# Moving the PSUM bank of the last narrow matmul chain of a fused gated mix

## The chip, the cores and the metric

One core of a Trainium2 chip runs the whole kernel. The metric is device time in microseconds (us), smaller is better; runs at full granted clock are compared with one another. The kernel before took 265.14 us (median of three runs, 265.03 to 265.6). Most of the argument reads the trace: the stretch from the first W4 matmul of the last tile to the end of the span, called "the tail stretch" below.

In the views PE stands for the matmuls of TensorE and PEld for its weight loads, DVE for VectorE, ACT for ScalarE, POOL for GpSimd, and SPq for the queue that issues the stores. PSUM is the memory that the matmuls of this kernel write; it is divided into banks. An "evacuation" is the VectorE instruction that reads a finished result from PSUM. A semaphore is a counter through which one engine waits for another.

## The reference

The reference mixes two branches with a sigmoid gate per row: linear attention over 32 heads, and a two-step MLP. What matters here is the end of the second branch and the mix, for S = 2048 rows, D = 640 columns and F = 1728 hidden columns in bfloat16:

```python
x1 = x + hs                                   # (S, 640)
h2 = _gelu(_layernorm(x1, axis=-1) @ w3) @ w4 # (S, 1728) @ (1728, 640)
b  = x1 + h2
return g * a + (1 - g) * b
```

## The kernel before

The kernel goes through the rows in four tiles of 512, and in each tile through four column groups `cc` (0 to 3) of the transposed hidden layer, each giving 128 output rows. One output has 128 x 640 float32; the kernel gives it a PSUM tile of two banks of 512 float32 each, a "pair". All PSUM tiles are such pairs, and their pool has four. Each output is computed as two parts, `hf` 0 and 1, one in each bank. The product with W4 sums over 13 full blocks of 128 hidden columns, and over a remainder of 64, which `w4_rest` computes for two groups at once in the two halves of the array (in the traces two such matmuls start 3 to 4 ns apart).

```python
ps = ctx.enter_context(tc.tile_pool(name="ps", bufs=4, space=PSUM))

def pair():
    return ps.tile([P, 2, 512], F32, name="pp")
# ... cut ...
LT = TS // 2                                                         # 256

def w4_dst(t, cc, pts, hf):
    n = D - TS if t == NT - 1 and cc % 2 else LT                     # 128 or 256
    return (pts[cc][:, 0, TS - n:TS], 0, n) if hf == 0 else (pts[cc][:, 1, 0:D - n], n, D)

def w4_mm(t, cc, pts, hf, start):
    dst, a, b = w4_dst(t, cc, pts, hf)
    for fc in range(FF):                                             # 13 blocks
        nc.tensor.matmul(dst, lhsT=st[t]["h2"][:, fc * TS + cc * P:fc * TS + (cc + 1) * P],
                         rhs=w4_sb[:, fc, a:b], start=start and fc == 0, stop=not start and fc == FF - 1)

def w4_part(t, cc, pts, hf):                                         # last tile, groups 1 and 3
    # ... cut: oc is one output tile per group ...
    nc.vector.scalar_tensor_tensor(oc[:, a:b], src, omg[:, c:c + 1], st[t]["x1"][cc][:, a:b],
                                   op0=ALU.mult, op1=ALU.add)
    nc.sync.dma_start(out2[c * P:(c + 1) * P, a:b], oc[:, a:b])

def w4_tile(t):
    pts = {cc: pair() for cc in (0, 2)}
    # ... cut: both parts of groups 0 and 2, without the remainder ...
    for cc in (1, 3):
        pts[cc] = pair()
    w4_rest(t, pts)                          # ends groups 0 and 2, starts groups 1 and 3
    # ... cut ...
    for cc in (0, 2):
        w4_out(t, cc, pts[cc])               # one evacuation and one store of 640 columns
    last = t == NT - 1
    for cc, hf in ((1, 1), (3, 1), (1, 0), (3, 0)) if last else ((1, 0), (1, 1), (3, 0), (3, 1)):
        # ... cut ...
        w4_mm(t, cc, pts, hf, False)
        if last:
            w4_part(t, cc, pts, hf)
        elif hf == 1:
            w4_out(t, cc, pts[cc])
```

In the last tile groups 1 and 3 are cut into a wide part of 512 columns and a narrow one of 128, and the two narrow parts come last, so that only 128 columns are left to evacuate and store behind the last matmul. "Chain" below means the 13 matmuls of one part.

Of the kernel before, what the change touches and what calls it, by code (L numbers as in the profile page):

```python
# [8 lines left out]
ALU = mybir.AluOpType  # L9
BF16 = mybir.dt.bfloat16  # L10
# [6 lines left out]
def kernel(  # L17
# [13 lines left out]
    nc = tc.nc  # L31
    P = 128
    S, D = A_x.shape[1], A_x.shape[2]
# [3 lines left out]
    TS = 512  # L37
    NT = S // TS
    CPT = TS // P
# [16 lines left out]
    out2 = out.rearrange("b s d -> (b s) d")  # L56
# [8 lines left out]
    outp = ctx.enter_context(tc.tile_pool(name="outp", bufs=2))  # L65
# [3 lines left out]
    def pair():  # L69
        return ps.tile([P, 2, 512], F32, name="pp")  # L70
# [25 lines left out]
    omg = const.tile([P, NCH], F32)  # L96
# [119 lines left out]
    for c in range(1, NCH):  # L216
        pt = pair()
# [175 lines left out]
    st = {}  # L393
# [30 lines left out]
    def x1_scale(t, cc):  # L424
        c = t * CPT + cc
        x1 = st[t]["x1"][cc]
        nc.scalar.activation(x1[:], x1[:], ACT.Copy, scale=omg[:, c:c + 1])
# [11 lines left out]
    LT = TS // 2  # L439
# [15 lines left out]
    def w3_rest(t, dst):  # L455
        for dc in range(DC):
            for v in range(2):
                nc.tensor.matmul(dst[FR * v:FR * (v + 1), :], lhsT=w3_sb[:, dc, FF * P:F],  # L458
                                 rhs=st[t]["lnT"][:, dc, v * LT:(v + 1) * LT], start=(dc == 0), stop=(dc == DC - 1))
        st[t]["h2x"] = h2x_p.tile([P, LT], BF16, name="h2x")  # L460
        nc.scalar.activation(st[t]["h2x"][:], dst, ACT.Gelu_apprx_tanh)  # L461

    def w4_dst(t, cc, pts, hf):
        n = D - TS if t == NT - 1 and cc % 2 else LT
        return (pts[cc][:, 0, TS - n:TS], 0, n) if hf == 0 else (pts[cc][:, 1, 0:D - n], n, D)

    def w4_mm(t, cc, pts, hf, start):
        dst, a, b = w4_dst(t, cc, pts, hf)
        for fc in range(FF):
            nc.tensor.matmul(dst, lhsT=st[t]["h2"][:, fc * TS + cc * P:fc * TS + (cc + 1) * P],  # L470
                             rhs=w4_sb[:, fc, a:b], start=start and fc == 0, stop=not start and fc == FF - 1)

    def w4_rest(t, pts):
        for u in range(2):
            for hf in range(2):
                for v in range(2):
                    rows = slice(FR * v, FR * (v + 1))
                    dst, a, b = w4_dst(t, u + 2 * v, pts, hf)
                    nc.tensor.matmul(dst, lhsT=st[t]["h2x"][rows, u * P:(u + 1) * P],  # L479
                                     rhs=w4_sb[rows, FF, a:b], start=u == 1, stop=u == 0)  # L480

    def w4_out(t, cc, pt):
        c = t * CPT + cc
        x1 = st[t]["x1"][cc]
        oc = outp.tile([P, D], BF16, name="oc")
        nc.vector.scalar_tensor_tensor(oc[:], pt[:].rearrange("p h e -> p (h e)")[:, TS - LT:TS - LT + D],  # L486
                                       omg[:, c:c + 1], x1[:], op0=ALU.mult, op1=ALU.add)
        nc.sync.dma_start(out2[c * P:(c + 1) * P, :], oc[:])

    ocs = {}  # L490

    def w4_part(t, cc, pts, hf):
        c = t * CPT + cc
        src, a, b = w4_dst(t, cc, pts, hf)
        if cc not in ocs:
            ocs[cc] = outp.tile([P, D], BF16, name="oc")
        oc = ocs[cc]
        nc.vector.scalar_tensor_tensor(oc[:, a:b], src, omg[:, c:c + 1], st[t]["x1"][cc][:, a:b],
                                       op0=ALU.mult, op1=ALU.add)
        nc.sync.dma_start(out2[c * P:(c + 1) * P, a:b], oc[:, a:b])  # L500

    def w4_tile(t):
        pts = {cc: pair() for cc in (0, 2)}
        for cc in (0, 2):
            if t + 1 < NT:
                x1_scale(t + 1, cc)
            for hf in range(2):
                w4_mm(t, cc, pts, hf, True)
        for cc in (1, 3):
            pts[cc] = pair()  # L510
        w4_rest(t, pts)
        if t + 1 < NT:
            w3_rest(t + 1, pts[0][:, 0, 0:LT])
        for cc in (0, 2):
            w4_out(t, cc, pts[cc])
        last = t == NT - 1
        for cc, hf in ((1, 1), (3, 1), (1, 0), (3, 0)) if last else ((1, 0), (1, 1), (3, 0), (3, 1)):
            if t + 1 < NT and hf == 0:
                x1_scale(t + 1, cc)
            w4_mm(t, cc, pts, hf, False)  # L520
            if last:
                w4_part(t, cc, pts, hf)
            elif hf == 1:
                w4_out(t, cc, pts[cc])

    for cc in range(CPT):
        w2_unit(0, cc)
# [19 lines left out]
    for t in range(NT):  # L547
        for i in range(NW3):
            w3_unit(t, i)
            if i < CPT and t + 1 < NT:  # L550
                w2_unit(t + 1, i)
            if 2 <= i < 2 + CPT:
                att_unit(t, i - 2)
        if t + 1 < NT:
            ln2_rstd(t + 1, 0, CPT)
            for cc in range(CPT):
                ln2_apply(t + 1, cc)
        if t == 0:
            w3_rest(0, pair()[:, 0, 0:LT])
        w4_tile(t)  # L560
# [30 lines left out]
```

## Time and profile before

| | kernel before |
|---|---|
| time, median of 3 | 265.14 us |
| span of the profiled run | 263.48 us |
| PE busy, share of the span | 98% |
| first W4 matmul of the last tile | 245.45 us |
| tail stretch | 18.03 us |

Lines of the page of the kernel before: busy time of the engines, the TensorE clock in tenths by slices of the span, and the chain of waits.

```profile
PE 258.4 (98%) x1722; PEld 161.0 (61%) x1740; DVE 141.4 (54%) x276; ACT 82.7 (31%) x123; POOL 20.2 (8%) x65
...
PEclk9999999999999999999999999999999999999999
...
PE 92%; SPq 3%; DMA 3%; issue 1%; DVE 0%
```

TensorE bounds the kernel: hardly any stage has a gap on PE. What can still be won lies in small gaps and in the serial tail behind the last matmul.

The timeline of the end of the kernel before. Columns: start, duration from the first start to the last end, engine, line, operation, output and inputs, shape, count, and in brackets the idle time before and what ended it. The timeline merges neighbours, so a row can hold other shapes than the one it names.

```profile
245.45 7.23 PE L470 MATMUL pp<-w_sb,h 128*128 128x256 bf16 x52
...
252.61 0.72 PE L479 MATMUL pp<-w_sb,h2x 64*128 64x256 bf16 x8
253.09 1.68 DVE L486 SCALAR_TENSOR_TENSOR oc<-pp,omg,x 128x640 bf16<-128x640 f32 x2 [7.57 <-PE pp L479]
253.26 6.39 PEld L470 LDWEIGHTS <-h 128*128 128x128 bf16 x40 [0.27 <-issue]
253.49 7.29 PE L470 MATMUL pp<-w_sb,h 128*128 128x512 bf16 x51 [0.16 <-issue]
254.00 1.12 SPq L488 DMA_DIRECT2D out_dram<-oc  x2
256.28 0.75 DVE L498 SCALAR_TENSOR_TENSOR oc<-pp,omg,x 128x512 bf16<-128x512 f32 x1 [1.51 <-PE pp L470]
257.06 4.46 SPq L500 DMA_DIRECT2D out_dram<-oc  x4
259.09 1.08 DVE L498 SCALAR_TENSOR_TENSOR oc<-pp,omg,x 128x512 bf16<-128x512 f32 x2 [2.05 <-PE pp L470]
259.89 0.71 PEld L470 LDWEIGHTS <-h 128*128 128x128 bf16 x12 [0.24 <-issue]
260.81 0.35 DVE L498 SCALAR_TENSOR_TENSOR oc<-pp,omg,x 128x128 bf16<-128x128 f32 x1 [0.65 <-PE pp L470]
```

Read the row at 259.89 first: the weight loads of the last chain stand idle for 0.24 us in the middle of otherwise dense work. By the records of the single instructions the matmuls of a 128-column chain start 56 ns apart, but the last chain's first one starts 336 ns after the one before it, 0.28 us late. It carries a semaphore wait on VectorE in the trace. The row at 259.09 holds two evacuations: that of group 3's wide part (0.75 us, ending at 259.84) and that of group 1's narrow part. The last chain starts 0.05 us after the first of the two ends. PE's own row shows no gap there, because the modelled end of one matmul overlaps the next starts.

The row at 253.49 names an idle 0.16 us that isn't one: it has 51 of 52 matmuls, and with the missing record put in at its place the starts are regular.

### The profile page before, as it was taken

The numbers are of one execution on the slowest core, as the hardware profiler recorded it, in microseconds if no ns is written. First come the engines' busy times: TensorE is split into PE (matmuls) and PEld (weight loads), VectorE is DVE, ScalarE is ACT, GpSimd is POOL, SyncE is SP. The second block draws the span as 40 slices with busy tenths as digits, with TensorE's granted clock in tenths as the row PEclk, the third lists the DMA queues.
The fourth block names the chain that finished last, engine by engine and source line by source line (L and its number), as shares of the span: only waits on it lengthen the run. The fifth ranks groups of instructions, "written<-read, shape, count | busy, mean of one in ns | idle before, by whom it ended". The sixth has DMA issues, their size and how long they took to land.

```text
span 263.5 us, 4244 instructions
## 1 busy us (share of the span) xinstructions
PE 258.4 (98%) x1722; PEld 161.0 (61%) x1740; DVE 141.4 (54%) x276; ACT 82.7 (31%) x123; POOL 20.2 (8%) x65
## 2 busy tenths in 40 slices
PE   8999999999999999999999999999999999999995
PEld 4767555688755644555667555667565577455743
DVE  1678778899947997955403464413356323112132
ACT  1555454321166236622502222412131332142100
POOL 5000050012210041001000001000001000000000
PEclk9999999999999999999999999999999999999999
DMA  7999988016672567700132000051100051100011
GB/s 191 175 193 370 374 261 322 0 27 124 124 99 57 101 111 172 248 0 2 25 75 77 25 0 2 0 100 52 50 0 2 0 101 52 50 0 2 0 50 50
DMA packets 46413, 24.14 MB, mean 92 GB/s; under 512 B 35770, under 2 KB 45626, under 8 KB 46394
## 3 DMA queue, kind: packets, MB, share of 16 engines
q1 hardware_dynamic: 45952, 23.39, 34.7%
q10 hardware_dynamic: 442, 0.49, 0.5%
q8 instruction: 13, 0.21, 0.3%
q14 instruction: 6, 0.05, 0.1%
HBM read 12.21 MB, written 2.62 MB: 56 GB/s over the span
## 4 chain that ended last, share of the span: by engine, by line
PE 92%; SPq 3%; DMA 3%; issue 1%; DVE 0%
PE pp L470 21%; PE pp L450 21%; PE pp L298 8%; PE pp L434 8%; PE pp L403 8%; PE pp L332 8%; PE pp L226 8%; PE pp L184 4%; DMA xT<-in_A_x_dram 3%; SPq L121 3%; PE pp L370 1%; PE pp L458 1%; PE pp L479 1%; PE pp L351 1%; PE pp L241 0%
## 5 line engine op out<-in xcount | busy, mean ns | idle before, releaser
L450 PE MATMUL pp<-lnxT,w_sb 128*128 128x512 bf16 x249 | 59.8, 379 | 0.6
L470 PE MATMUL pp<-w_sb,h 128*128 128x256 bf16 (+3 forms) x415 | 57.8, 299 | 0.3 <-issue 0.2
L452 ACT ACTIVATE h<-pp 128x1024 bf16<-128x1024 f32 (+1 forms) x28 | 26.9, 962 | 82.2 <-PE pp L450 82.2
L470 PEld LDWEIGHTS <-h 128*128 128x128 bf16 x416 | 39.3, 98 | 18.0 <-issue 1.3
L450 PEld LDWEIGHTS <-w_sb 128*128 128x128 bf16 x260 | 25.5, 98 | 26.8
L486 DVE SCALAR_TENSOR_TENSOR oc<-pp,omg,x 128x640 bf16<-128x640 f32 x14 | 12.0, 881 | 41.4 <-ACT h2x L461 21.3
L437 DVE SCALAR_TENSOR_TENSOR x<-pp,gate,x 128x640 f32<-128x640 f32 x16 | 13.9, 867 | 29.4 <-PE pp L434 29.4
L176 ACT ACTIVATE e<-pp 128x640 bf16<-128x640 f32 (+1 forms) x26 | 21.5, 827 | 9.5 <-PE pp L226 9.5
L434 PE MATMUL pp<-m_sb,pqT 128*128 128x320 bf16 x160 | 24.3, 299 | 0.0
L403 PE MATMUL pp<-w_sb,hsT 128*128 128x320 bf16 x160 | 23.9, 299 | 0.0
L406 DVE TENSOR_TENSOR x<-pp,x_sb 128x640 f32<-128x640 f32 x16 | 13.1, 820 | 19.7 <-PE pp L403 19.6
L184 PE MATMUL pp<-wk_sb,xT 128*128 128x320 bf16 (+1 forms) x160 | 22.7, 300 | 0.3 <-DMA wk_sb<-in_A_wqkv_dram 0.2
L298 PE MATMUL pp<-x_sb,pk 128*128 128x320 bf16 (+1 forms) x160 | 22.3, 300 | 0.0
L226 PE MATMUL pp<-xT,hsT 128*128 128x512 bf16 x98 | 21.6, 379 | 0.1
L298 PEld LDWEIGHTS <-pk 128*128 128x128 bf16 x160 | 18.8, 117 | 3.5
L403 PEld LDWEIGHTS <-hsT 128*128 128x128 bf16 x160 | 15.7, 98 | 8.2
L434 PEld LDWEIGHTS <-pqT 128*128 128x128 bf16 x160 | 15.7, 98 | 7.7
L184 PEld LDWEIGHTS <-xT 128*128 128x128 bf16 x160 | 15.4, 98 | 6.9 <-DMA xT<-in_A_x_dram 0.7
L332 PE MATMUL pp<-lnxT,w_sb 128*128 128x512 bf16 x76 | 17.9, 379 | 0.2
L226 PEld LDWEIGHTS <-hsT 128*128 128x128 bf16 x100 | 11.8, 118 | 9.7
L268 POOL TENSOR_SCALAR rstd<-mv 128x4 f32<-128x4 f32 (+1 forms) x11 | 3.4, 312 | 153.6 <-DVE mv L274 153.6
L177 DVE TENSOR_SCALAR e<-e 128x640 bf16<-128x640 bf16 (+1 forms) x26 | 9.5, 367 | 8.9 <-ACT e L176 7.5
(72 smaller groups left out, 195.0 us busy)
## 6 DMA issues: line engine op xcount, KB each, us to landing
out_dram<-oc SPq DMA_DIRECT2D x14, 160.0 KB, 1.8
w_sb<-in_B_w_dram SPq DMA_DIRECT2D x1, 2160.0 KB, 8.8
w_sb<-in_B_w_dram SPq DMA_DIRECT2D x1, 2080.0 KB, 10.0
x_sb<-in_A_x_dram SPq DMA_DIRECT2D x1, 1280.0 KB
x_sb<-in_A_x_dram SPq DMA_DIRECT2D x1, 1120.0 KB, 8.2
wo_sb<-in_A_wo_dram SPq DMA_DIRECT2D x6, 160.0 KB, 7.7
hsT<-in_A_wqkv_dram SPq DMA_DIRECT2D x1, 800.0 KB, 5.6
m_sb<-in_A_wqkv_dram SPq DMA_DIRECT2D x1, 800.0 KB, 12.8
```

The costliest lines, as they stand in the source:

```text
L176: nc.scalar.activation(ev, src, ACT.Exp)
L184: nc.tensor.matmul(pt[:, hf, 0:n], lhsT=xT[:, dc, c * P:(c + 1) * P], rhs=wk_sb[:, dc, hf * HD:hf * HD + n], start=(dc == 0), stop=(dc == ...
L226: nc.tensor.matmul(pt[:, t % 2, :], lhsT=wq_sb[:, dc, :].rearrange("p (m j) -> p j m", j=DC)[:, j], rhs=xT[:, dc, t * TS:(t + 1) * TS], st ...
L298: nc.tensor.matmul(pt[:, hf, 0:HD + hf], lhsT=w, rhs=x_sb[:, c, hf * HD:(hf + 1) * HD + hf], start=(c == 0), stop=(c == NCH - 1))
L332: nc.tensor.matmul(pt[:, i, :], lhsT=w, rhs=lnxT[t][:, dc, :], start=(dc == 0), stop=(dc == DC - 1))
L403: nc.tensor.matmul(pt[:, hf, 0:HD], lhsT=hsT[:, fc, 2 + c * P:2 + (c + 1) * P], rhs=w2_sb[:, fc, hf * HD:(hf + 1) * HD], start=(fc == 0), ...
L406: nc.vector.tensor_tensor(x1[:].rearrange("p (h e) -> p h e", h=2), pt[:, :, 0:HD], x_sb[:, c, 0:D].rearrange("p (h e) -> p h e", h=2), op ...
L434: nc.tensor.matmul(pt[:, hf, 0:HD], lhsT=pqT[:, j, c * P:(c + 1) * P], rhs=m_sb[:, j, hf * HD:(hf + 1) * HD], start=(j == 0), stop=(j == D ...
L437: nc.vector.scalar_tensor_tensor(x1, pt[:, :, 0:HD], gate[:, c:c + 1], x1, op0=ALU.mult, op1=ALU.add)
L450: nc.tensor.matmul(pt[:, k, :], lhsT=w3_sb[:, dc, fc * P:(fc + 1) * P], rhs=lnT[:, dc, :], start=(dc == 0), stop=(dc == DC - 1))
L452: nc.scalar.activation(h2[:, 2 * i * TS:(2 * i + n) * TS], pt[:].rearrange("p h e -> p (h e)")[:, 0:n * TS], ACT.Gelu_apprx_tanh)
L470: nc.tensor.matmul(dst, lhsT=st[t]["h2"][:, fc * TS + cc * P:fc * TS + (cc + 1) * P], rhs=w4_sb[:, fc, a:b], start=start and fc == 0, stop ...
```

## The change

The intent is that the last narrow part (group 3's) gets a bank in a pair whose other bank was evacuated long before, so that its chain has nothing to wait for. To make room, groups 0 and 2 of the last tile are cut 512 + 128 as well, and their parts are spread over three pairs: 0 holds group 0's wide part, 1 group 2's wide and group 0's narrow part, 2 group 3's wide and group 2's narrow part, and group 3's narrow part goes to pair 0. Group 1 has pair 3 for itself. The core of the diff, shortened:

```diff
-    def w4_dst(t, cc, pts, hf):
-        n = D - TS if t == NT - 1 and cc % 2 else LT
-        return (pts[cc][:, 0, TS - n:TS], 0, n) if hf == 0 else (pts[cc][:, 1, 0:D - n], n, D)
+    NW = D - TS
+    def w4_tiles(t, ccs, pts):
+        if t < NT - 1:
+            # ... cut: one pair per group, 256 + 384 columns, as before ...
+        else:
+            for _ in range(3 if 0 in ccs else 1):
+                pts["pairs"] = pts.get("pairs", []) + [pair()]
+            homes = {0: (0, 1), 2: (1, 2)} if 0 in ccs else {1: (3, 3), 3: (2, 0)}
+            for cc, (w, n) in homes.items():
+                wide, narrow = pts["pairs"][w][:, 0, :], pts["pairs"][n][:, 1, 0:NW]
+                pts[cc, 0], pts[cc, 1] = (narrow, 0, NW), (wide, NW, D)
# ... cut ...
+    def w4_out(t, cc, pts):
+        oc = outp.tile([P, D], BF16, name="oc")
+        if t < NT - 1:
+            w4_stt(t, cc, oc, pts[cc], 0, D)
+        else:
+            for hf in range(2):
+                w4_stt(t, cc, oc, *pts[cc, hf])
+        w4_store(t, cc, oc, 0, D)
# ... cut, in w4_tile, for groups 0 and 2 ...
-            for hf in range(2):
+            for hf in (1, 0):
                 w4_mm(t, cc, pts, hf, True)
```

So groups 0 and 2 of the last tile need two evacuations each instead of one, and in all tiles their wider part is computed first.

More of the change, by code (lines that the diff above doesn't have):

```diff
@@ L461, in w3_rest @@
         nc.scalar.activation(st[t]["h2x"][:], dst, ACT.Gelu_apprx_tanh)
-    def w4_dst(t, cc, pts, hf):
-        n = D - TS if t == NT - 1 and cc % 2 else LT
-        return (pts[cc][:, 0, TS - n:TS], 0, n) if hf == 0 else (pts[cc][:, 1, 0:D - n], n, D)
+    NW = D - TS
+    def w4_tiles(t, ccs, pts):
+        if t < NT - 1:
+            for cc in ccs:
+                pt = pair()
+                pts[cc, 0], pts[cc, 1] = (pt[:, 0, TS - LT:TS], 0, LT), (pt[:, 1, 0:D - LT], LT, D)
+                pts[cc, "rest"] = pt[:, 0, 0:LT]
+                pts[cc] = pt[:].rearrange("p h e -> p (h e)")[:, TS - LT:TS - LT + D]
+        else:
[5 more added lines that the diff above has]
+                pts[cc, 0], pts[cc, 1] = (narrow, 0, NW), (wide, NW, D)
     def w4_mm(t, cc, pts, hf, start):
-        dst, a, b = w4_dst(t, cc, pts, hf)
+        dst, a, b = pts[cc, hf]
         for fc in range(FF):
@@ L477, in w4_rest, with w4_stt @@
                     rows = slice(FR * v, FR * (v + 1))
-                    dst, a, b = w4_dst(t, u + 2 * v, pts, hf)
+                    dst, a, b = pts[u + 2 * v, hf]
                     nc.tensor.matmul(dst, lhsT=st[t]["h2x"][rows, u * P:(u + 1) * P],
                                      rhs=w4_sb[rows, FF, a:b], start=u == 1, stop=u == 0)
-    def w4_out(t, cc, pt):
+    def w4_stt(t, cc, oc, src, a, b):
         c = t * CPT + cc
-        x1 = st[t]["x1"][cc]
-        oc = outp.tile([P, D], BF16, name="oc")
-        nc.vector.scalar_tensor_tensor(oc[:], pt[:].rearrange("p h e -> p (h e)")[:, TS - LT:TS - LT + D],
-                                       omg[:, c:c + 1], x1[:], op0=ALU.mult, op1=ALU.add)
-        nc.sync.dma_start(out2[c * P:(c + 1) * P, :], oc[:])
@@ L490, with w4_store @@
-    ocs = {}
-    def w4_part(t, cc, pts, hf):
-        c = t * CPT + cc
-        src, a, b = w4_dst(t, cc, pts, hf)
-        if cc not in ocs:
-            ocs[cc] = outp.tile([P, D], BF16, name="oc")
-        oc = ocs[cc]
         nc.vector.scalar_tensor_tensor(oc[:, a:b], src, omg[:, c:c + 1], st[t]["x1"][cc][:, a:b],
                                        op0=ALU.mult, op1=ALU.add)
+    def w4_store(t, cc, oc, a, b):
+        c = t * CPT + cc
         nc.sync.dma_start(out2[c * P:(c + 1) * P, a:b], oc[:, a:b])
+    def w4_out(t, cc, pts):
[6 more added lines that the diff above has]
+        w4_store(t, cc, oc, 0, D)
@@ L502, in w4_tile @@
     def w4_tile(t):
-        pts = {cc: pair() for cc in (0, 2)}
+        last = t == NT - 1
+        pts = {}
+        w4_tiles(t, (0, 2), pts)
         for cc in (0, 2):
-            if t + 1 < NT:
+            if not last:
                 x1_scale(t + 1, cc)
-            for hf in range(2):
+            for hf in (1, 0):
                 w4_mm(t, cc, pts, hf, True)
-        for cc in (1, 3):
-            pts[cc] = pair()
+        w4_tiles(t, (1, 3), pts)
         w4_rest(t, pts)
-        if t + 1 < NT:
-            w3_rest(t + 1, pts[0][:, 0, 0:LT])
+        if not last:
+            w3_rest(t + 1, pts[0, "rest"])
@@ L514, in w4_tile @@
         for cc in (0, 2):
-            w4_out(t, cc, pts[cc])
-        last = t == NT - 1
+            w4_out(t, cc, pts)
+        ocs = {}
         for cc, hf in ((1, 1), (3, 1), (1, 0), (3, 0)) if last else ((1, 0), (1, 1), (3, 0), (3, 1)):
-            if t + 1 < NT and hf == 0:
+            if not last and hf == 0:
                 x1_scale(t + 1, cc)
@@ L521, in w4_tile @@
             if last:
-                w4_part(t, cc, pts, hf)
+                if hf == 1:
+                    ocs[cc] = outp.tile([P, D], BF16, name="oc")
+                w4_stt(t, cc, ocs[cc], *pts[cc, hf])
+                w4_store(t, cc, ocs[cc], *pts[cc, hf][1:])
             elif hf == 1:
-                w4_out(t, cc, pts[cc])
+                w4_out(t, cc, pts)
     for cc in range(CPT):
```

## The prediction

> **What bounds the kernel now.** TensorE: PE is busy 258.4 of a span of 263.5 us (98%, the page), the granted clock is full in every slice, and the chain of waits is 92% PE. The change touches the W4 stage, almost only its last tile, from 245.45 us to the end. So it can move little.
>
> **The wait it removes.** In the timeline of the last tile four chains of 13 matmuls end the kernel: 512 columns of column group 1, 512 of group 3, then 128 of 1 and 128 of 3. The last chain should start at 259.555 + 0.056 = 259.61 us. It starts at 259.89; the weight loads show 0.24 us idle before it. VectorE evacuates group 3's 512 columns from 259.09 to 259.84, and the chain starts 0.05 us after that. The evacuation reads the other bank of the pair that the chain writes. The Trainium skill, "PSUM — Partial Sum Buffer", Summary: rules for kernel authors, asks only for a different bank when PSUM is read while a matmul runs. So I take the wait for tracking by pair, not for a need of the hardware. It costs 0.28 us, all on the chain. After the change that chain writes the second bank of the pair of group 0's wide part, evacuated around 254 us, so it should not wait.
>
> **What it adds and moves.**
> - Groups 0 and 2 of the last tile are cut 128 + 512 instead of 256 + 384. Starts are 109 and 163 ns apart at 256 and 384: 272 ns per 640 columns either way. The Trainium skill, "TensorE: Matmul & The Clock Gate", Back-to-back issue gap, has columns over 2.4 GHz plus 2.5 ns; the trace agrees (56, 109, 163, 216 ns). Neutral.
> - Remainder matmuls (64 rows, two at once): the first pair took 120 ns at 256 columns, held by the second weight load (96 ns). At 128 columns it still takes about 120, while the next pair grows from 162 to 216. Cost 0.05 us, on the chain.
> - Groups 0 and 2 are evacuated by four instructions instead of two: 2 x (0.75 + 0.35) = 2.2 instead of 1.75 us. VectorE then ends near 255.4; its next work waits for PE until 256.28. Group 0's store, whose buffer group 1 reuses, lands near 256.05 instead of 255.8. Off the chain.
> - In tiles 0 to 2 only the order of the two parts changes: about 0.
>
> **Sum.** -0.28 + 0.05 = -0.23 us; what follows the last matmul (evacuation 0.35 us, store 1.45 us to landing, end of program) slides along. The store queue is free in time (260.68). Prediction 264.9 us, inside the spread of the three runs. Range 264.5 to 265.4. Faster by over 2%: 0.005; within 2%: 0.985; slower by over 2%: 0.01.
>
> **What would show it.** The last narrow chain starts 56 ns after the previous matmul, while the evacuation of group 3's wide part still runs; the 0.24 us idle of the weight loads is gone; four evacuations follow the remainder matmuls; from the last chain's end to the span's end it is still about 2.7 us; tiles 0 to 2 are unchanged.
>
> **What would make it wrong.** The tracking finds another reader of the shared pair, so the wait stays or moves; group 0's evacuation delays group 1's; the last two stores, now closer, slow each other; noise hides 0.2 us.

## The result, and the profile after

The changed kernel took 265.09, 265.31 and 265.02 us in the three runs at full clock; the kernel before had 265.31 us as the median of its four. The ratio is 0.9993, with a 95% interval of 0.9974 to 1.0013. A ratio here is the mean time of one kernel's fast runs over that of the other's of the same rounds, so not quite the ratio of the medians. In a later session (run r1_after_again) the medians were 264.75 and 265.27 us, the ratio 0.9987 (0.9974 to 0.9999). "The same" at 2% is certain; time alone doesn't show the direction: run r2_wait_back, which has the wait again, has nearly the same ratio (0.9989).

A fourth run, the profiled one, took 458.19 us: the mean granted clock was 0.561 in it. It is left out of all comparisons, and the profile after is that of r1_after_again, the same kernel at full clock (264.75 us, span 263.04 us). Its lines that answer to the page before:

```profile
PE 259.5 (99%) x1740; PEld 160.4 (61%) x1740; DVE 141.6 (54%) x278; ACT 82.7 (31%) x123; POOL 20.2 (8%) x65
...
PEclk9999999999999999999999999999999999999999
...
PE 99%; DVE 0%; issue 0%
```

PE's busy time looks 1.1 us longer, but all 1740 matmuls are recorded here and 1722 were before, so the two can't be compared. Nor is the step from 92% to 99% of PE in the chain of waits a gain of the change: the runs r5_after_near and r6_rest_wide_first, whose end is that of the changed kernel, show 92% again.

The timeline of its end:

```profile
252.45 0.72 PE L492 MATMUL pp<-w_sb,h2x 64*128 64x128 bf16 x8
252.94 1.93 DVE L497 SCALAR_TENSOR_TENSOR oc<-pp,omg,x 128x128 bf16<-128x128 f32 x4 [7.57 <-PE pp L492]
253.09 7.07 PEld L483 LDWEIGHTS <-h 128*128 128x128 bf16 x52 [0.26 <-issue]
253.10 7.24 PE L483 MATMUL pp<-w_sb,h 128*128 128x512 bf16 x52
253.98 7.11 SPq L502 DMA_DIRECT2D out_dram<-oc  x6
256.12 0.75 DVE L497 SCALAR_TENSOR_TENSOR oc<-pp,omg,x 128x512 bf16<-128x512 f32 x1 [1.25 <-PE pp L483]
258.92 1.08 DVE L497 SCALAR_TENSOR_TENSOR oc<-pp,omg,x 128x512 bf16<-128x512 f32 x2 [2.05 <-PE pp L483]
260.38 0.35 DVE L497 SCALAR_TENSOR_TENSOR oc<-pp,omg,x 128x128 bf16<-128x128 f32 x1 [0.38 <-PE pp L483]
```

The 52 weight loads behind the remainder matmuls are now one row with no break; before, the row broke after 40 of them. The evacuation of group 3's wide part still runs from 258.92 to 259.67, but the last chain starts at 259.45, inside it, and its first matmul carries no semaphore wait in the trace. VectorE's idle time before the last evacuation falls from 0.65 to 0.38 us.

The tail stretch of the two, as windows over the trace: first the kernel before, then the changed one. Columns: the window, its length, then busy time and count of PE, PEld, DVE, ACT and POOL, the granted clock, the DMA share and GB/s.

```profile
245.45:263.48 18.03, 15.05 (x112) 9.33 (x111) 3.93 (x7) 0.60 (x1) 0.00 (x0) 1.00 0.11 36
```

```profile
245.29:263.04 17.75, 15.05 (x113) 8.24 (x111) 4.18 (x9) 0.60 (x1) 0.00 (x0) 1.00 0.11 37
```

It is 0.28 us shorter: 18.026 against 17.746 us from the unrounded starts. That PE is busy for 15.05 us in both is a coincidence: in the kernel before the missing record takes 0.16 us away, and the modelled end of the matmul before the wait adds as much (of the 0.28 us of wait only 0.12 us show as idle). The rest of the difference of the spans, 0.16 us, was already there when the first W4 matmul of the last tile started (245.45 against 245.29).

Where runs differ by chance can be read too. Over the eight fast profiles the stretch from the last matmul of the first stage (the keys, which waits for the first loads) to the first W3 matmul took 76.3 us in each, within 0.02 us. The start of that stretch lay anywhere from 27.06 to 27.73 us. So chance moves the beginning by 0.67 us, more than twice the effect, while the end repeats to about 0.02 us.

### The profile page after: what moved, and what is told of

Read it like the earlier page. It is cut to its first block, busy times and chain, and to the rows that moved or that the text cites. A ratio compares the mean times of both kernels' runs of the same rounds, so it can differ in the third digit from the quotient of the medians.

```text
span 456.5 us, 4245 instructions
## 1 busy us (share of the span) xinstructions
PE 449.4 (98%) x1721; PEld 213.6 (47%) x1740; DVE 143.2 (31%) x278; ACT 83.3 (18%) x123; POOL 19.9 (4%) x65
## 4 chain that ended last, share of the span: by engine, by line
PE 98%; issue 1%; DVE 0%
PE pp L483 22%; PE pp L450 21%; PE pp L403 8%; PE pp L184 8%; PE pp L298 8%; PE pp L434 8%; PE pp L226 8%; PE pp L332 8%; PE pp L370 1%; PE pp L196 1%; PE pp L458 1%; PE pp L492 1%; PE pp L351 1%; PE pp L241 0%; PE pp L205 0%
## 5 line engine op out<-in xcount | busy, mean ns | idle before, releaser
L450 PE MATMUL pp<-lnxT,w_sb 128*128 128x512 bf16 x249 | 102.9, 584 | 2.0 <-issue 0.9
L483 PE MATMUL pp<-w_sb,h 128*128 128x384 bf16 (+3 forms) x414 | 100.3, 436 | 0.5 <-issue 0.5
L483 PEld LDWEIGHTS <-h 128*128 128x128 bf16 x416 | 52.0, 130 | 48.8 <-issue 39.6
L450 PEld LDWEIGHTS <-w_sb 128*128 128x128 bf16 x260 | 35.0, 135 | 58.2 <-issue 53.5
L497 DVE SCALAR_TENSOR_TENSOR oc<-pp,omg,x 128x640 bf16<-128x640 f32 (+2 forms) x20 | 14.5, 748 | 94.2 <-ACT h2x L461 42.4
L434 PE MATMUL pp<-m_sb,pqT 128*128 128x320 bf16 x160 | 41.5, 439 | 0.0
L403 PE MATMUL pp<-w_sb,hsT 128*128 128x320 bf16 x160 | 41.2, 437 | 0.0
L184 PE MATMUL pp<-wk_sb,xT 128*128 128x320 bf16 (+1 forms) x160 | 39.5, 440 | 0.0
L298 PE MATMUL pp<-x_sb,pk 128*128 128x320 bf16 (+1 forms) x160 | 38.8, 439 | 0.0
L226 PE MATMUL pp<-xT,hsT 128*128 128x512 bf16 x98 | 38.3, 582 | 0.3
L332 PE MATMUL pp<-lnxT,w_sb 128*128 128x512 bf16 x76 | 30.8, 580 | 0.9 <-issue 0.7
L332 PEld LDWEIGHTS <-w_sb 128*128 128x128 bf16 x80 | 10.2, 130 | 19.0 <-issue 18.5
```

Of the source, the lines that this page charges most:

```text
L184: nc.tensor.matmul(pt[:, hf, 0:n], lhsT=xT[:, dc, c * P:(c + 1) * P], rhs=wk_sb[:, dc, hf * HD:hf * HD + n], start=(dc == 0), stop=(dc == ...
L226: nc.tensor.matmul(pt[:, t % 2, :], lhsT=wq_sb[:, dc, :].rearrange("p (m j) -> p j m", j=DC)[:, j], rhs=xT[:, dc, t * TS:(t + 1) * TS], st ...
L298: nc.tensor.matmul(pt[:, hf, 0:HD + hf], lhsT=w, rhs=x_sb[:, c, hf * HD:(hf + 1) * HD + hf], start=(c == 0), stop=(c == NCH - 1))
L332: nc.tensor.matmul(pt[:, i, :], lhsT=w, rhs=lnxT[t][:, dc, :], start=(dc == 0), stop=(dc == DC - 1))
L403: nc.tensor.matmul(pt[:, hf, 0:HD], lhsT=hsT[:, fc, 2 + c * P:2 + (c + 1) * P], rhs=w2_sb[:, fc, hf * HD:(hf + 1) * HD], start=(fc == 0), ...
L434: nc.tensor.matmul(pt[:, hf, 0:HD], lhsT=pqT[:, j, c * P:(c + 1) * P], rhs=m_sb[:, j, hf * HD:(hf + 1) * HD], start=(j == 0), stop=(j == D ...
```

## Experiments

The theory: the wait isn't a need of the hardware. The program orders accesses to a PSUM tile by the whole tile, so a chain into one bank of a pair waits for the reading of the other bank. The wait ends when that evacuation ends. Taking it away is worth its full 0.28 us, as nothing else follows. Rivals: the gain is given back behind the last matmul; the shapes matter and not the pair; passing a pair from VectorE to PE has a fixed price; the two banks of a pair can't be used at once. All runs gave correct results at full clock (0.998 to 1.0), and all are timed beside the kernel before.

| run | tail stretch, us | gap between the matmul starts in question | time, median us | ratio to before (95%) |
|---|---|---|---|---|
| kernel before | 18.03 | 336 ns (56 is regular) | 265.27 / 265.21 | 1 |
| r1_after_again | 17.75 | 56 ns | 264.75 | 0.9987 (0.9974 to 0.9999) |
| r2_wait_back | 18.03 | 335 ns | 264.99 | 0.9989 (0.9976 to 1.0001) |
| r3_place_only | 17.75 | 56 ns | 265.07 | 0.9988 (0.9976 to 1.0001) |
| r4_before_near | 18.76 | 1219 ns (216 is regular) | 266.04 | 1.0026 (1.0013 to 1.0040) |
| r5_after_near | 17.76 | 216 ns | 265.08 | 0.9991 (0.9978 to 1.0005) |
| r6_rest_wide_first | 17.75 | 56 ns | 264.68 | 0.9981 (0.9967 to 0.9995) |
| r7_single_banks | 17.75 | 56 ns | 265.75 | 1.0018 (1.0003 to 1.0034) |

The gap is that from the start of the last matmul before the chain that could wait to the start of the chain's first one. The first four runs shared one session, the last three another, on another chip, hence two medians of the kernel before. The tail stretch of r7_single_banks begins behind a wait that this run adds (below).

### r1_after_again: the changed kernel, unchanged

> The changed kernel again, for a profile at full clock (its first one ran at a granted clock of 0.561). Theory (the wait came from tracking by pair; now gone): the last narrow chain follows the chain before it 56 ns apart, the 0.24 us idle of the weight loads is gone, and the stretch from the first W4 matmul of the last tile to the end of the span is 18.03 - 0.23 = 17.80 us (before: 245.45 to 263.48). Time ratio 0.999. Rival (the gain is given back behind the last matmul, in VectorE or the stores): the wait is gone but the stretch stays within 0.05 us of 18.03, with the last evacuation or the last store waiting longer.

Shown above. The wait is gone and the tail stretch is 0.28 us shorter, which is all of the wait; the 0.05 us that I had set against it is not there. From the end of the last matmul to the end of the span both kernels take 2.70 us, so nothing is given back behind it.

Building the kernels again, without running them, shows which evacuation was waited for. In the kernel before, the first matmul of the last chain writes one bank of group 3's pair and waits until VectorE has counted the evacuation of the other bank. In the changed kernel it waits for nothing. A wait of this kind is left on group 3's wide chain, which shares a pair with group 2's narrow part, but that evacuation ended at 254.21 us and the chain starts at 255.92.

### r2_wait_back: one placement undone

```diff
-            homes = {0: (0, 1), 2: (1, 2)} if 0 in ccs else {1: (3, 3), 3: (2, 0)}
+            homes = {0: (0, 1), 2: (1, 0)} if 0 in ccs else {1: (3, 3), 3: (2, 2)}
```

> The changed kernel with one thing undone: group 3's narrow part shares a pair with group 3's wide part again, group 2's narrow part with group 0's wide one. Theory: only the wait comes back, 0.28 us, so the stretch is 17.80 + 0.28 = 18.08 us, slightly above the kernel before because the 0.05 us of the remainder matmuls stay. Rival (the new shapes and four evacuations, not the shared pair, set the end): the stretch stays at that of the changed kernel.

The tail stretch was 18.03 us, the one of the kernel before, with the gap of 335 ns. Its timeline has the idle weight loads again, with the number from before:

```profile
258.58 1.07 DVE L497 SCALAR_TENSOR_TENSOR oc<-pp,omg,x 128x512 bf16<-128x512 f32 x2 [2.05 <-PE pp L483]
...
259.39 0.71 PEld L483 LDWEIGHTS <-h 128*128 128x128 bf16 x12 [0.24 <-issue]
260.31 0.35 DVE L497 SCALAR_TENSOR_TENSOR oc<-pp,omg,x 128x128 bf16<-128x128 f32 x1 [0.65 <-PE pp L483]
```

So neither the new cut nor the four evacuations set the end; which pair group 3's narrow part lies in does. The size was expected 0.05 us too high, for the same missing cost. In time this run can't be told from r1_after_again (0.9989 and 0.9987): the first 28 us hide it.

### r3_place_only: the kernel before, with the placement alone

```diff
     def w4_dst(t, cc, pts, hf):
         n = D - TS if t == NT - 1 and cc % 2 else LT
+        if t == NT - 1 and cc == 3 and hf == 0:
+            return pts[2][:, 1, D - LT:TS], 0, n
```

> The kernel before with nothing but the placement changed: group 3's narrow part goes into the spare 128 columns of the second bank of group 2's pair; the 256 + 384 split and single evacuations stay. Theory: the wait is gone and the 0.05 us in the remainder matmuls is not paid, so the stretch is 18.03 - 0.28 = 17.75 us. Rival (a shared bank costs, or group 2's evacuation now waits for more): above 17.80 us.

The tail stretch was 17.75 us: two lines give the whole gain of the change, without new shapes or evacuations. In its timeline the weight loads of the two narrow chains run through while the wide part is evacuated:

```profile
258.90 1.44 PEld L472 LDWEIGHTS <-h 128*128 128x128 bf16 x25
259.11 1.08 DVE L500 SCALAR_TENSOR_TENSOR oc<-pp,omg,x 128x512 bf16<-128x512 f32 x2 [2.06 <-PE pp L472]
...
260.56 0.35 DVE L500 SCALAR_TENSOR_TENSOR oc<-pp,omg,x 128x128 bf16<-128x128 f32 x1 [0.37 <-PE pp L472]
```

A first form of this experiment, which put the part into group 0's pair, was refused by the check for races ahead of any run: matmuls of two row halves of the array would have written one bank with nothing to order them. The Trainium skill, "PSUM — Partial Sum Buffer", PSUM bank collisions raise a hardware error, has that rule: different row tiles can't access the same bank at the same time. Group 2 uses the same row half as group 3, so its bank was allowed. No run here shows the collision itself.

### r4_before_near and r5_after_near: the wait made longer

In both kernels, the same edit brings group 3's narrow chain straight behind its wide one:

```diff
-        for cc, hf in ((1, 1), (3, 1), (1, 0), (3, 0)) if last else ...
+        for cc, hf in ((1, 1), (3, 1), (3, 0), (1, 0)) if last else ...
```

> The kernel before with the last two narrow chains in the other order, so that group 3's narrow chain comes straight after its wide one. Theory (the wait lasts until the evacuation of the wide part ends): the chain that could start at 258.89 waits until 259.89, 1.0 us instead of 0.28, and the stretch is 18.03 + 0.73 = 18.76 us; ratio 1.0027. Rival (a fixed price of about 0.28 us for handing a pair from VectorE to PE): the stretch stays at 18.03 us.

> The changed kernel with the last two narrow chains in the other order, as in the run r4_before_near. Theory: no chain waits for the evacuation of group 3's wide part, so the order costs nothing: stretch 17.75 us as the changed kernel measured, 1.01 us below r4_before_near (18.76); ratio to the kernel before 0.999. Rival (the changed kernel only moves the wait to another chain, which this order exposes): a gap above 0.1 us before one of the narrow chains and a stretch above 17.85 us.

The timeline of r4_before_near:

```profile
259.23 0.75 DVE L498 SCALAR_TENSOR_TENSOR oc<-pp,omg,x 128x512 bf16<-128x512 f32 x1 [2.06 <-PE pp L470]
260.00 2.39 SPq L500 DMA_DIRECT2D out_dram<-oc  x3
260.03 1.61 PE L470 MATMUL pp<-w_sb,h 128*128 128x128 bf16 x26 [0.84 <-DVE oc L498]
260.03 1.44 PEld L470 LDWEIGHTS <-h 128*128 128x128 bf16 x25 [1.12 <-issue]
```

Now the gap is long enough to show on PE too, and the view names its cause: the chain waited for VectorE's evacuation, which ended at 259.98. The start was 1219 - 216 ns = 1.00 us late, and the tail stretch grew by 0.73 us, as expected. A fixed price of 0.28 us would have left it unchanged: that rival is out. With the same order the changed kernel has no gap and a tail stretch of 17.76 us:

```profile
258.62 2.05 PE L483 MATMUL pp<-w_sb,h 128*128 128x512 bf16 x28
258.84 1.65 PEld L483 LDWEIGHTS <-h 128*128 128x128 bf16 x26
259.25 1.08 DVE L497 SCALAR_TENSOR_TENSOR oc<-pp,omg,x 128x512 bf16<-128x512 f32 x2 [2.05 <-PE pp L483]
260.03 1.38 SPq L502 DMA_DIRECT2D out_dram<-oc  x3
260.70 0.35 DVE L497 SCALAR_TENSOR_TENSOR oc<-pp,omg,x 128x128 bf16<-128x128 f32 x1 [0.38 <-PE pp L483]
```

This pair shows the effect in time as well: 1.0026 (1.0013 to 1.0040) without the change, 0.9991 (0.9978 to 1.0005) with it, each against the kernel before in its own session. The intervals don't overlap, and the difference, 0.0035 of 265 us or 0.9 us, fits the 1.00 us between the tail stretches.

### r6_rest_wide_first: what the remainder matmuls really cost

```diff
     def w4_rest(t, pts):
         for u in range(2):
-            for hf in range(2):
+            for hf in (1, 0):
```

> The changed kernel with the remainder matmuls' wide part first. My prediction held that the second weight load keeps the first pair at 120 ns whatever its width; the changed kernel showed 67 ns at 128 columns. If pairs are limited by their columns plus about 11 ns (new reading): first pair 216 + 11 = 227 ns, second 56 ns, remainder stage and stretch unchanged within 0.02 us of 17.75 us. If a weight load limits the start as I predicted: stretch 0.05 us shorter.

From the first pair's start to the second's the records show 227 ns, then 55 ns to the third; the tail stretch stayed at 17.75 us. The timelines of three kernels have the same duration for these eight matmuls, whatever the width of the pair that comes first. The kernel before had 256 columns first and 0.72 us, the changed kernel 128 columns first and 0.72 us (both shown above), and this run 512 columns first:

```profile
252.37 0.72 PE L492 MATMUL pp<-w_sb,h2x 64*128 64x512 bf16 x8
```

So the first pair costs its columns and 11 ns: 67, 120 and 227 ns at 128, 256 and 512 columns. My cost of 0.05 us doesn't exist. The ratio of this run, 0.9981, is no gain over r1_after_again: the intervals overlap and the tails are equal.

### r7_single_banks: the same neighbouring banks, tracked one by one

```diff
-    ps = ctx.enter_context(tc.tile_pool(name="ps", bufs=4, space=PSUM))
+    s_ps = ExitStack()
+    ps = s_ps.enter_context(tc.tile_pool(name="ps", bufs=4, space=PSUM))
# ... cut; ahead of the last w4_tile ...
+            s_ps.close()
+            ps1 = ctx.enter_context(tc.tile_pool(name="ps1", bufs=8, space=PSUM))
+            banks = [ps1.tile([P, 1, 512], F32, name="pb") for _ in range(8)]
# ... cut; in w4_tiles, for the last tile ...
+            for cc in ccs:
+                wide, narrow = banks.pop(0)[:, 0, :], banks.pop(0)[:, 0, 0:NW]
+                pts[cc, 0], pts[cc, 1] = (narrow, 0, NW), (wide, NW, D)
```

> The changed kernel, but in its last tile every part has a tile of one bank for itself, taken from a second pool that takes over the space of the pairs; group 3's wide and narrow parts lie in neighbouring banks, as in a pair of the kernel before. Theory (the wait is tracking by pair, no need of the hardware): the last narrow chain follows 56 ns after the chain before, while VectorE reads the neighbouring bank, and the result is correct. Rival (the two banks of a pair can't be written and read at once, or the tracking orders neighbouring banks too): a wait of 0.28 us before the last chain. Taking over the space may cost a wait of up to 0.9 us before the first W4 matmul of the tile, which counts for neither.

Group 3's two parts lie in neighbouring banks again, as in the kernel before, but each is a tile of its own. (A build of this kernel places them in banks 2 and 3; the pair of the kernel before was banks 4 and 5.) The timeline:

```profile
245.48 0.60 ACT L453 ACTIVATE h<-pp 128x512 bf16<-128x512 f32 x1 [1.41 <-PE pp L451]
246.13 7.22 PE L481 MATMUL pb<-w_sb,h 128*128 128x512 bf16 x51 [0.69 <-ACT h L453]
...
253.93 7.07 PEld L481 LDWEIGHTS <-h 128*128 128x128 bf16 x52 [0.26 <-issue]
...
259.76 1.08 DVE L495 SCALAR_TENSOR_TENSOR oc<-pb,omg,x 128x512 bf16<-128x512 f32 x2 [2.06 <-PE pb L481]
260.54 1.39 SPq L500 DMA_DIRECT2D out_dram<-oc  x3
261.21 0.35 DVE L495 SCALAR_TENSOR_TENSOR oc<-pb,omg,x 128x128 bf16<-128x128 f32 x1 [0.38 <-PE pb L481]
```

The 52 weight loads run without a break while VectorE reads the neighbouring bank, and the result is correct. So the wait isn't needed here; the tracking by tile makes it. The kernel as a whole is slower (1.0018), for a reason seen in the second row: to take over the space of the pairs, the first W4 matmul waits until ScalarE has read the last W3 result, which by the build lies in other banks (4 and 5; the matmul writes bank 0). The start comes 1065 - 216 ns = 0.85 us late. The same kind of tracking, of a whole pool, costs more here than the wait that it removes.

No experiment pointed to a version that beats both kernels beyond the change itself: r1, r3, r5 and r6 end in the same tail stretch within 0.015 us.

## Why the prediction was right, point by point

- **The time.** I predicted 264.9 us, between 264.5 and 265.4; the medians were 265.2 and, in the other session, 264.75 us. "Within 2%" was right. The hit says little about the mechanism: the range is wide enough to hold the median of the kernel before as well (265.14 and 265.31), so it would have held without any effect. The predicted -0.23 us was too small to be shown by these times; the trace showed -0.28 us.
- **The wait.** It was where and as long as I read it (336 - 56 = 280 ns), on the critical path in full (r1, r2, r3), and due to the tracking of the pair (r4, r7, and the waits in the built programs).
- **The term that was mis-sized.** "Remainder matmuls (64 rows, two at once): the first pair took 120 ns at 256 columns, held by the second weight load (96 ns)... Cost 0.05 us." I took the coincidence of 120 ns with a weight load of 96 ns for a cause. The first pair took 67 ns at 128 columns, and the stage as a whole 0.72 us in both kernels. In the changed kernel a weight load recorded as starting at 252.460 and taking 96 ns had its matmul start at 252.516, 40 ns before the load's end. The Trainium skill, "TensorE: Matmul & The Clock Gate", Architectural detail, says that a matmul can begin before the weight load completes; the trace agrees, and I had not used it. With this term at zero the sum is -0.28 us, as measured.
- **Equal work for other cuts.** 512 + 128 columns took as long as 384 + 256: from the first W4 matmul of the last tile to the first remainder matmul it was 7.159 us in both kernels.
- **Tiles 0 to 2.** They are unchanged, as predicted: from the first W3 matmul to the first W4 matmul of the last tile it was 141.57 us in both kernels.
- **Evacuations and buffers.** I expected four evacuations to take 2.2 instead of 1.75 us; they took 1.93 instead of 1.68 us, because the next one starts before the previous one has ended by the records. Group 1's wide evacuation was still released by PE (idle 1.25 us, ended by the matmuls), not by group 0's store, which landed at 255.75 us and not at 256.05. So this stayed off the path as predicted.
- **The tail behind the last matmul.** 2.70 us in both kernels, as predicted.

## What to carry to other kernels

When a tile spans several PSUM banks, look for the start of a chain that follows an evacuation of *another* bank of the same tile by some 50 ns: here that was a wait by tile. It cost the rest of that evacuation, and it went away when the part that is written late shared a tile with a part that is read early. At the end of this kernel the gap was worth its full length. Measure effects of this size over a stretch of the trace that starts behind the noisy part, here a few tenths of a microsecond over the last 18 us, and make the suspected wait longer by an experiment if the times are to show it.

## What the Trainium skill lacked or had wrong

- "TensorE: Matmul & The Clock Gate", Back-to-back issue gap, gives a sustained spacing of about 81 ns at 128 columns and about 131 ns at 512 for streams with a weight load ahead of each matmul. It calls its own formula, columns over 2.4 GHz plus 2.5 ns, one for isolated matmuls. In all runs here, with a weight load for every matmul and at full clock, the spacing was 56 and 216 ns, as that formula has it.
- The same page, Part 1, knows granted clocks of 4/8, 8/8 and 13/16, the last with three or more busy cores on a die, and events that read 1/4. One run of this one-core kernel had a mean of 0.561 over 456.5 us (PEclk at 5 tenths in all but the first slice), with the starts of 512-column matmuls 401 or 402 ns apart in 355 cases and 307 or 308 ns in 83. Starting the same kernel again gave 1.0. None of its cases fits (at 4/8 it has 426.7 ns for 512 columns), and the runs don't show the cause.
- No page has a time for the change from full matmuls to half-height ones; "TensorEngine Tiling (Array Packing)", Tiling Modes, says only that changing the tiling mode drains TensorE. The records show the time: the start of the first 64-row matmul comes 258 ns after a full one of 384 columns, where 163 is regular, and 152 ns after one of 128 columns, where 56 is regular. It is about 95 ns at either width. The change back takes as much: in r1_after_again the first full matmul starts 312 ns after a 64-row one of 512 columns, where 216 is regular.
- "PSUM — Partial Sum Buffer", Summary: rules for kernel authors, rightly asks for guarding by bank. It doesn't warn that a program may guard a tile of two banks as one: that cost 0.28 us in the kernel before, 1.00 us in r4_before_near, and nothing in r7_single_banks, where two neighbouring banks were separate tiles.
